# Attention, routing and two FFNs on one core: where spare weights are converted, when raw tiles are asked for, and how one-hot places are laid out

## Chip, cores and metric

One core of a Trainium2 chip. The metric is device time in microseconds of one execution; lower is better. The kernel before has a median of 944.61 us over three runs (944.56 to 945.29).

## The reference, cut to what matters

Three stages follow each other on 2304 tokens of 512 features.

```python
# 1. attention: 4 batches x 8 heads, 512 local and 32 global tokens, head size 64;
#    local queries see a window of +-32 keys and all global ones, global queries see everything
x = attention(q_l, k_l, v_l, q_g, k_g, v_g)          # -> [2304, 512]
# 2. mixture of 8 experts, 288 tokens each, greedy over all (token, expert) logits, largest first
logits = x @ w_gate
for idx in argsort(-logits.flatten()):
    tok, e = idx // 8, idx % 8
    if assigned[tok] < 0 and counts[e] < 288: assigned[tok] = e; counts[e] += 1
out[assigned == e] = relu(x[assigned == e] @ w1[e]) @ w2[e]      # w1: 512x1024, w2: 1024x512
# 3. gated FFN on every token, hidden size 1536
return (silu(x @ w_gate) * (x @ w_val)) @ w_out
```

All inputs and the output are fp32.

## The kernel before

**Matmuls.** In the FFN stages each fp32 product is made of three fp32r matmuls (`mm3`, L1000 to L1002): a weight tile is split into a high and a low part, and so is the activation; high x high, high x low and low x high are accumulated. The split of a weight tile of 128 x 1024 is done in `parts`: ScalarE copies the raw tile into the high half (L971) and VectorE subtracts it from the raw tile for the low half (L972). Tokens of an expert come as 272 + 16: 272 columns per matmul in the products (`TE`), the 16 left over of each expert are gathered in `rest`.

**Attention (`attention`).** 40 units (4 local blocks of 128 queries and one global unit for each half batch) run in a software pipeline: slot `n` issues the scores of unit `n`, the exponentials of `n-1`, the transposes of `n-2` and the product with V of `n-3`. Three more slots drain it. At the end of slots 3 and 6 to 42 the slot calls `cv.step()`, `int(CVA*(n+1)) - int(CVA*n)` times (`CV0`, `CV1`).

**Conversion (`Convert`).** The third stage's weights are 36 pieces of 128 x 1024 words. Each is read (`cv_raw`, 512 KB), packed by ScalarE (L116, `cv_a`) and three VectorE operations (L122 to L124, `cv_f`) and stored into a DRAM buffer `wd` (256 KB), from which the FFN reads it later. A generator walks through the pieces; a step is either the first VectorE operation of a piece (cost 0.6) or its other two (cost 1.2), with the loads, the ScalarE operation and the store of neighbouring pieces before or after them. In attention pieces 0 to `NC`-1 are converted, with three loads ahead (`LD`) and 5, 3 and 4 buffers. `second`, called between attention and the experts, runs whatever steps are left and then sets up pieces `NC` to 35 with one load ahead and two buffers of each kind (`rest_of`). In the FFN each `tick` adds `CV2` to a budget, once expert 1 has its tokens, and steps are taken while the budget is positive:

```python
s.cvw += n                                   # n = CV2, in convert()
while s.cvw > 0 and not s.cv.finished:
    s.cvw -= s.cv.step()
```

**Experts and FFN (`Ffn`).** `moe(k)` runs expert `k`: 8 blocks `h` of the first product and 6 of 8 blocks `y` of the second, each 12 matmuls and one tick, then 48 matmuls without a tick. `group(g)` runs the gated FFN for two experts at once: 12 blocks with four ticks of 12 matmuls each, then the output product with 512 columns per matmul (12 or 13 ticks). The order is expert 0, 1, group 0, expert 2, 3, group 1 and so on. A tick also takes the next steps of `bgen`, which interleaves the routing of the next experts (`Router.phase`), the gathers of their tokens (`fetch`) and the clean-up after each.

**Weight tiles.** All tiles stand in one list of 136 in order of use: 8 for each expert, 12 for `g` and `v`, 6 for `o`. `w` calls `pump(m)` when tile `m` is used: tiles up to `m` that are not yet split are split now; then at most one more is split ahead, up to `LOOK` = 4 past `m`, if it is `here`: asked at least `LAG` ticks ago, and for an expert's tile its routing finished. Then `load` asks for raw tiles: while fewer than `RAWS` past the next tile to be split are under way. There are `RAWS` = 4 raw buffers, and SyncE issues all these DMAs in program order, those of the conversion among them. Before the first expert three tiles are asked for (`LA0`).

```python
return m in s.raw and s.ticks - s.asked[m] >= LAG and (kind in "gvo" or s.done_phase >= k)
```

**Routing (`Router.phase`).** For each expert six rounds narrow down a threshold; a round is a comparison on VectorE (L677), 17 matmuls with one-hot weights `ohr` (L684) and some small VectorE operations. Then each chosen token gets a place. The place's low 7 bits become a one-hot row of 128 for each of 17 chunks: a comparison of an iota with the places on VectorE (L731), with the chunk innermost in memory (`ol` is [128, 128, 18]; `iota2` repeats the iota so that both operands are bf16), in two pieces of 8 and 10 chunks. 17 matmuls use `ol[:, :, c]`, a column step of 18 elements, as weights (L735) and give the token numbers, by which GpSimd gathers the rows (L872).

Of the kernel before, what the change touches and what calls it, by code (L numbers as in the profile page):

```python
# [9 lines left out]
F32 = mybir.dt.float32  # L10
F32R = mybir.dt.float32r
BF16 = mybir.dt.bfloat16
I32 = mybir.dt.int32
AF = mybir.ActivationFunctionType
ALU = mybir.AluOpType
# [10 lines left out]
NCH = 17  # L26
# [33 lines left out]
class Ctx: pass  # L60


CVA = 1.45
VW = 3
CV0, CV1 = 3, 6
QB = 8
PL = 2
RAWB, CB, FB, LD = 5, 3, 4, 3
NC = 24
EN = 36  # L70
UO, LW = 0, 39
ORD, KQN = 'hc4vgq56w', 2
# [2 lines left out]
class Convert:  # L75

    def __init__(s, tc, t, wd, pool):
        s.nc, s.t, s.wd = tc.nc, t, wd
        s.use(pool, RAWB, CB, FB)
        s.jobs = []  # L80
        for j in range(6):
            for nm in ("moe2_w_gate", "moe2_w_val"):
                s.jobs += [(nm, j, h) for h in range(2)]
        for j in range(6):
            s.jobs += [("moe2_w_out", j, h) for h in range(2)]
        s.raw, s.a, s.f = {}, {}, {}
        s.stored, s.finished = -1, False
        s.g = s.gen(0, NC, LD, False)

# [3 lines left out]
    def rest_of(s, pool):  # L93
# [3 lines left out]
        s.finished = False  # L97
        s.g = s.gen(NC, 36, 1, True)

    def load(s, n):  # L100
        nm, j, h = s.jobs[n]
        w = s.t[nm].bitcast(I32)
        raw = s.pool.tile([128, 512, 2], I32, name="cv_raw", bufs=s.rawb)
        if nm == "moe2_w_out":
            src = w[256 * j + 128 * h:256 * j + 128 * h + 128, :]
            dst = raw.rearrange("p n u -> p (n u)")
        else:
            src = w[256 * h:256 * h + 256, 512 * j:512 * j + 512].rearrange("(c p) f -> p c f", p=128)
            dst = raw.rearrange("p (c n) u -> p c (n u)", c=2)
        s.nc.sync.dma_start(dst, src)  # L110
        s.raw[n] = raw
# [52 lines left out]
def attention(tc, ctx, t, cv=None, consts=None, early=None):  # L164
    nc = tc.nc
    K = ctx
    with tc.tile_pool(name="a_c", bufs=1) as cp_, tc.tile_pool(name="a_w", bufs=3) as wp_, \
# [298 lines left out]
        for n in range(N + 3):  # L466
# [54 lines left out]
            if cv and n >= CV1:  # L521
                for _ in range(int(CVA * (n + 1)) - int(CVA * n)):
                    cv.step()
# [18 lines left out]
class Router:  # L542

    def __init__(s, tc, K, pool, bank=None):
        s.tc, s.nc, s.K, s.bank = tc, tc.nc, K, bank
        s.known = -1
        t = lambda shape, dt, name: pool.tile(shape, dt, name="r_" + name)
        s.pen = t([128, E], F32, "pen"); s.need = t([128, E], F32, "need"); s.nd = t([128, 1], F32, "nd"); s.sel8 = t([128, E], F32, "sel8")
        s.cap = t([128, E], F32, "cap"); s.w8 = t([128, E], F32, "w8"); s.w8p = t([128, 1], F32, "w8p")
        s.tk = t([128, NCH], F32, "tk"); s.ac = t([128, NCH], F32, "ac")  # L550
        s.Lm = t([128, NCH, E], F32, "Lm"); s.v = t([128, NCH], F32, "v"); s.v0 = t([128, NCH], F32, "v0")
        s.eq = t([128, NCH, E], F32, "eq")

        s.ohr = t([128, NCH, 4, 32], BF16, "ohr"); s.oh = s.ohr[:, :, 0, 0:E]
        s.T = t([128, KM], F32, "T"); s.io = [t([128, r, k], BF16, f"io{i}") for i, (k, r) in enumerate(KN)]; s.Td = t([128, max(k * r for k, r in KN)], F32, "Td"); s.cmp = t([128, NCH, KM], BF16, "cmp")
        s.ge = t([128, KM], BF16, "ge"); s.ke = t([128, 1], F32, "ke"); s.k1 = [t([128, 1], F32, f"k1{i}") for i in range(2)]
        s.onesb = t([128, 128], BF16, "onesb"); s.tri = t([128, 128], BF16, "tri"); s.iota = t([128, 128], F32, "iota")
        s.lo2 = [t([128, 1], F32, f"lo{i}") for i in range(2)]; s.k2 = t([128, 1], F32, "k2"); s.cd = t([128, 1], F32, "cd"); s.hi = t([128, 1], F32, "hi"); s.gmin = t([128, 1], F32, "gmin")
        s.mm = t([128, 2], F32, "mm"); s.mt = t([128, 2], F32, "mt")
        s.m1 = t([128, 1], F32, "m1"); s.d = t([128, 1], F32, "d"); s.ew = t([128, 1], F32, "ew"); s.em = t([128, 1], F32, "em")  # L560
        s.c8 = t([128, E], BF16, "c8"); s.e8 = t([128, E], F32, "e8"); s.ohe = t([128, E], F32, "ohe")
        s.eis = [t([128, 1], I32, f"ei{e}") for e in range(E)]; s.M = t([128, 2, NCH], F32, "M"); s.Mb = t([128, 2 * NCH], BF16, "Mb")
        s.ones = t([128, 2 * NCH], F32, "ones"); s.Pc = t([128, 2 * NCH + 2], BF16, "Pc")
        s.lo = t([128, NCH], I32, "lo"); s.thr = t([128, 4], F32, "thr")
        s.acc = t([128, NCH], F32, "acc"); s.pp = t([128, NCH], I32, "pp")
        s.hb = t([128, 4, NCH], F32, "hb"); s.h3 = t([128, 3, NCH], F32, "h3"); s.ol = t([128, 128, NCH + 1], BF16, "ol"); s.iota2 = t([128, 128, NCH + 1], BF16, "iota2"); s.lob = t([128, NCH + 1], BF16, "lob"); s.rid = t([128, NCH, 2], BF16, "rid")
        s.rh = t([128, NCH, 3, 2], BF16, "rh"); s.A = t([128, NCH], F32, "A"); s.G = t([128, NCH], F32, "G")
        s.idxf = [t([128, 3], F32, f"idxf{e}") for e in range(E)]
        s.idx = [t([128, 3], I32, f"idx{e}") for e in range(E)]
# [82 lines left out]
    def phase(s, n):  # L652
        nc, V, K, b = s.nc, s.nc.vector, s.K, s.bank
# [61 lines left out]
        p = b[:, 320:354]  # L715
# [4 lines left out]
        V.scalar_tensor_tensor(s.pp, s.M[:, 0], -1.0, s.M[:, 1], op0=ALU.add, op1=ALU.add)  # L720
        W = nc.gpsimd if n == 0 else V
        V.tensor_scalar(s.lo, s.pp, 127, None, op0=ALU.bitwise_and)
        V.tensor_copy(s.lob[:, 0:NCH], s.lo)
        V.tensor_tensor(s.hb, s.pp[:, None, :].to_broadcast([128, 4, NCH]), s.thr[:, :, None].to_broadcast([128, 4, NCH]), op=ALU.is_ge)
        yield 1, 0.0
        W.tensor_tensor(s.h3, s.hb[:, 0:3], s.hb[:, 1:4], op=ALU.subtract)
# [1 line left out]
                        s.rid[:, :, None, :].to_broadcast([128, NCH, 3, 2]), op=ALU.mult)  # L728
        for c0, c1 in ((0, 8), (8, NCH + 1)):
            yield 1, 0.0  # L730
            V.tensor_tensor(s.ol[:, :, c0:c1], s.iota2[:, :, c0:c1], s.lob[:, None, c0:c1].to_broadcast([128, 128, c1 - c0]), op=ALU.is_equal)  # L731
        yield TQ, 0.0
        q = b[:, 384:390]
        for c in range(NCH):
            nc.tensor.matmul(q, s.ol[:, :, c], s.rh[:, c].rearrange("p k u -> p (k u)"), start=c == 0, stop=c == NCH - 1)  # L735
        q3 = q.rearrange("p (k u) -> p k u", u=2)
        V.tensor_copy(s.idxf[n], q3[:, :, 1])
        V.scalar_tensor_tensor(s.idx[n], q3[:, :, 0], 16.0, s.idxf[n], op0=ALU.mult, op1=ALU.add)
# [25 lines left out]
TE = CAP  # L764
OT = 4
GW, GL = 6, 12
CV2 = 0.75
LA0 = 3
MO = 1
YT = 0  # L770
GROUPS = [[0, 1], [2, 3], [4, 5], [6, 7]]
WB, LOOK, RAWS, LAG = 6, 4, 4, 2
class Ffn:
    def __init__(s, tc, K, R, pool, banks, t):
        s.tc, s.nc, s.K, s.R, s.t, s.pool = tc, tc.nc, K, R, t, pool
# [138 lines left out]
    def tick(s):  # L914
        s.ticks += 1
        if 1 in s.ready:
            s.convert(CV2)
        if s.wait > 0:
# [72 lines left out]

    def load(s):
        s.nd = max(s.nd, s.np)
        while s.nd < min(s.np + RAWS, len(s.tiles)) and s.known(s.nd):
            s.dma(s.nd)
            s.nd += 1

# [212 lines left out]
```

## Time and profile before

| | us |
|---|---|
| median of three runs | 944.61 |
| the profiled execution | 943.54 |
| its span | 941.7 |
| attention ends, last copy of the logits (L527) | 172.7 |
| first matmul of expert 0 | 205.5 |
| expert 1's first product with a split tile, on the chain of waits | 251.7 |
| expert 1's last eviction (L1050) ends | 292.7 |
| the last conversion operation on VectorE ends | 343.2 |

| engine | busy us | share of the span |
|---|---|---|
| TensorE, matmuls | 858.6 | 91% |
| VectorE | 590.9 | 63% |
| ScalarE | 394.0 | 42% |
| GpSimd | 107.2 | 11% |

Times in the trace are counted from the start of the span. Rows by stretch give the busy times in the order TensorE matmuls, TensorE weight loads, VectorE, ScalarE, GpSimd. In the trace's names PE is TensorE, PEld its weight loads, DVE is VectorE, ACT ScalarE, POOL GpSimd and SP SyncE; b are the PSUM banks, rbank the router's. The shares are means over stages with different limits, so the profile is read by stretch: how much of a stretch TensorE was busy, what the other engines did in it, and which waits ended last. A TensorE clock of 1.00 is 2.4 GHz; the lower of the two levels, 1.2 GHz, shows as 0.50, and a mean over a stretch that has both lies between.

### The profile page before, as it was taken

What the parts mean: (1) busy time and instruction counts of PE and PEld (TensorE: products, weight loads), DVE (VectorE), ACT (ScalarE), POOL (GpSimd) and SP (SyncE); (2) the same over time, 40 slices, a digit from 0 to 9 for tenths busy, and PEclk for the clock granted to TensorE, in tenths of its full rate; (3) what the DMA queues carried; (4) which work ended last, traced back from release to release, by engine and by line L of the source; (5) the groups of instructions that cost most, each with busy time, mean ns of one, the idle gap of its engine ahead of it and who ended that gap; (6) DMA issues with size and microseconds to landing.
All of it is one profiled execution on the core that took longest, in us unless ns stands there. A gap on an engine that the chain in (4) does not pass through costs nothing.

```text
span 941.7 us, 19213 instructions
## 1 busy us (share of the span) xinstructions
PE 858.6 (91%) x7567; PEld 794.8 (84%) x7567; DVE 590.9 (63%) x1489; ACT 394.0 (42%) x823; POOL 107.2 (11%) x189
## 2 busy tenths in 40 slices
PE   6999999448688678999999999999999999999997
PEld 5888887348588678978999889899999889999985
DVE  3678777678787687756896877355554336644410
ACT  4888887122343332323443233244443234533300
POOL 5444230010100100102100000110100020000002
PEclk9999999759699789999999999999999999999999
DMA  7988994041576532233651312365412435522101
GB/s 172 242 243 247 265 286 130 33 159 59 167 236 224 180 124 87 73 114 132 183 175 53 110 46 85 127 194 174 140 56 84 131 114 179 157 90 90 46 1 56
DMA packets 109386, 128.62 MB, mean 137 GB/s; under 512 B 57392, under 2 KB 75056, under 8 KB 109296
## 3 DMA queue, kind: packets, MB, share of 16 engines
q1 hardware_dynamic: 105856, 118.35, 41.2%
q0 software_dynamic: 2896, 8.92, 2.7%
q8 instruction: 59, 0.97, 0.4%
q14 instruction: 31, 0.25, 0.1%
q10 hardware_dynamic: 544, 0.13, 0.1%
HBM read 109.02 MB, written 18.35 MB: 135 GB/s over the span
## 4 chain that ended last, share of the span: by engine, by line
PE 53%; issue 20%; DVE 15%; DMA 4%; ACT 4%; POOL 1%; SPq 1%; POOLq 0%; DVEq 0%; ACTq 0%
PE b L1000 9%; PE b L1002 8%; PE b L1001 8%; PE b L1105 4%; PE b L1106 4%; PE b L1107 4%; DVE wHL L972 3%; PE s L303 3%; DMA wd<-cv_f 3%; DVE r_cmp L677 2%; PE tr L323 2%; PE o L334 2%; PE o L339 1%; PE tr L269 1%; PE tr L358 1%
## 5 line engine op out<-in xcount | busy, mean ns | idle before, releaser
L1000 PE MATMUL b<-yH,wHL 128*128 128x272 f32 x768 | 229.1, 298 | 0.4 <-DVE yL L1050 0.4
L1002 PE MATMUL b<-yH,wHL 128*128 128x272 f32 x768 | 225.2, 293 | 0.0
L1001 PE MATMUL b<-yL,wHL 128*128 128x272 f32 x768 | 224.7, 293 | 0.0
L972 DVE TENSOR_TENSOR wHL<-raw,wHL 128x1024 fp32r<-128x1024 f32 x136 | 163.8, 1222 | 45.0 <-ACT wHL L971 44.9
L971 ACT CAST wHL<-raw 128x1024 fp32r<-128x1024 f32 x136 | 139.2, 1047 | 79.3 <-PE b L1107 52.2
L1000 PEld LDWEIGHTS b<-yH,wHL 128*128 128x128 f32 x768 | 148.7, 194 | 8.5 <-issue 7.7
L1001 PEld LDWEIGHTS b<-yL,wHL 128*128 128x128 f32 x768 | 149.1, 194 | 0.0
L1002 PEld LDWEIGHTS b<-yH,wHL 128*128 128x128 f32 x768 | 148.6, 193 | 0.0
L1083 ACT CAST dH<-b 128x272 fp32r<-128x272 f32 x96 | 37.1, 386 | 187.5 <-DVE b L1082 187.5
L1082 DVE TENSOR_TENSOR b<-b,si 128x272 f32<-128x272 f32 x96 | 42.8, 446 | 55.8 <-PE b L1002 55.7
L1000 PE MATMUL b<-dH,wHL 128*128 128x272 f32 x256 | 76.1, 297 | 1.7 <-ACT dH L1027 1.7
L1000 PE MATMUL b<-xH,wHL 128*128 128x272 f32 x252 | 75.2, 298 | 1.6 <-DVE dL L1028 0.8
L1105 PE MATMUL b<-wHL,dH 128*128 128x512 f32 x192 | 76.4, 398 | 0.0
L1001 PE MATMUL b<-dL,wHL 128*128 128x272 f32 x256 | 74.7, 292 | 1.7 <-DVE dL L1028 1.7
L1002 PE MATMUL b<-xH,wHL 128*128 128x272 f32 x252 | 74.0, 294 | 2.2 <-DVE wHL L972 2.2
L1107 PE MATMUL b<-wHL,dH 128*128 128x512 f32 x192 | 75.9, 395 | 0.0
L1106 PE MATMUL b<-wHL,dL 128*128 128x512 f32 x192 | 75.9, 395 | 0.0
L1002 PE MATMUL b<-dH,wHL 128*128 128x272 f32 x256 | 74.5, 291 | 0.0
L1001 PE MATMUL b<-xL,wHL 128*128 128x272 f32 x252 | 73.4, 291 | 0.0
L1084 DVE TENSOR_TENSOR dL<-b,dH 128x272 fp32r<-128x272 f32 x96 | 42.4, 442 | 43.5 <-ACT dH L1083 43.5
L1027 ACT ACTIVATE dH<-b 128x272 fp32r<-128x272 f32 x64 | 25.4, 397 | 95.5 <-PE b L1002 89.4
L872 POOL DMA_INDIRECT xg<-xd,r_idx x24 | 22.8, 949 | 309.5 <-DVE r_idxf L739 123.1
(236 smaller groups left out, 1610.8 us busy)
## 6 DMA issues: line engine op xcount, KB each, us to landing
raw<-wd SPq DMA_DIRECT2D x72, 512.0 KB, 3.6
raw<-moe_w SPq DMA_DIRECT2D x64, 512.0 KB, 4.0
wd<-cv_f SPq DMA_DIRECT2D x36, 256.0 KB, 5.4
cv_raw<-moe_w_gate SPq DMA_DIRECT2D x12, 512.0 KB, 4.7
cv_raw<-moe_w_val SPq DMA_DIRECT2D x12, 512.0 KB, 5.8
cv_raw<-moe_w_out SPq DMA_DIRECT2D x12, 512.0 KB, 6.6
xd<-xt SPq DMA_DIRECT2D x16, 256.0 KB, 4.6
st<-k_l SPq DMA_DIRECT2D x28, 128.0 KB, 4.8
```

The lines of the kernel that those rows point to most:

```text
L303: nc.tensor.matmul(s[:, u, 160 * a:160 * a + 160], qT[n % 2][:, a, 2 * g + u].rearrange("d h q -> d (h q)"), kT[n % 2][:, a, o:o + 160], s ...
L971: nc.scalar.copy(w[:, 0], raw)
L972: nc.vector.tensor_tensor(w[:, 1], raw, w[:, 0].bitcast(F32), op=ALU.subtract)
L1000: nc.tensor.matmul(out, wH, xH, start=start, stop=False)
L1001: nc.tensor.matmul(out, wH, xL, start=False, stop=False)
L1002: nc.tensor.matmul(out, wL, xH, start=False, stop=stop)
L1082: nc.vector.tensor_tensor(b, b, si, op=ALU.mult)
L1083: nc.scalar.copy(dH[:, f, :], b)
L1084: nc.vector.tensor_tensor(dL[:, f, :], b, dH[:, f, :].bitcast(F32), op=ALU.subtract)
L1105: nc.tensor.matmul(ob[i], dh, H[:, f % 2, :], start=f == 0, stop=False)
L1106: nc.tensor.matmul(ob[i], dl, H[:, f % 2, :], start=False, stop=False)
L1107: nc.tensor.matmul(ob[i], dh, L[:, f % 2, :], start=False, stop=f == 11)
```

## The change

Seven constants and conditions and the layout of one tile are changed. Attention takes 1.65 conversion steps per slot and converts 30 of the 36 pieces; the FFN takes 0.4 budget units per tick. A raw tile must have been asked for four ticks ago to be split ahead, and `load` asks up to two tiles past the next one to be split and not three; the number of raw buffers stays. For experts 1 to 7 the one-hot places are written with the place innermost (`olc`, a view of the same memory), from the fp32 iota and the int32 places, in pieces of 8 and 9 chunks, and the matmuls read contiguous weights; the bf16 copy of the places (`lob`) is made for expert 0 only.

```diff
-CVA = 1.45
+CVA = 1.65
-NC = 24
+NC = 30
...
+        s.olc = s.ol.rearrange("p w c -> p (w c)")[:, 0:NCH * 128].rearrange("p (c w) -> p c w", w=128)
...
-        V.tensor_copy(s.lob[:, 0:NCH], s.lo)
+        if n == 0:
+            V.tensor_copy(s.lob[:, 0:NCH], s.lo)
...
-            V.tensor_tensor(s.ol[:, :, c0:c1], s.iota2[:, :, c0:c1], s.lob[:, None, c0:c1].to_broadcast([128, 128, c1 - c0]), op=ALU.is_equal)
+            if n == 0:
+                V.tensor_tensor(s.ol[:, :, c0:c1], s.iota2[:, :, c0:c1], s.lob[:, None, c0:c1].to_broadcast([128, 128, c1 - c0]), op=ALU.is_equal)
+            else:
+                x = slice(c0, min(c1, NCH))
+                N = x.stop - c0
+                V.tensor_tensor(s.olc[:, x], s.iota[:, None, :].to_broadcast([128, N, 128]), s.lo[:, x, None].to_broadcast([128, N, 128]), op=ALU.is_equal)
...
-            nc.tensor.matmul(q, s.ol[:, :, c], s.rh[:, c].rearrange("p k u -> p (k u)"), start=c == 0, stop=c == NCH - 1)
+            nc.tensor.matmul(q, s.olc[:, c] if n else s.ol[:, :, c], s.rh[:, c].rearrange("p k u -> p (k u)"), start=c == 0, stop=c == NCH - 1)
...
-CV2 = 0.75
+CV2 = 0.4
-WB, LOOK, RAWS, LAG = 6, 4, 4, 2
+WB, LOOK, RAWS, LAG = 6, 4, 4, 4
...
-        while s.nd < min(s.np + RAWS, len(s.tiles)) and s.known(s.nd):
+        while s.nd < min(s.np + RAWS - 1, len(s.tiles)) and s.known(s.nd):
```

## Rows read from the trace of the kernel before

**Rows 1.** stretches: length, busy us of each engine, granted clock, DMA share, GB/s

```profile
20.00:146.70 126.70, 125.90 (x1699) 108.60 (x1700) 93.44 (x213) 108.91 (x295) 45.86 (x89) 1.00 0.88 251
...
205.50:251.70 46.20, 35.38 (x346) 33.06 (x346) 39.09 (x135) 13.81 (x23) 2.77 (x3) 0.83 0.26 82
...
251.70:292.70 41.00, 35.67 (x307) 34.28 (x308) 34.24 (x90) 20.27 (x31) 0.00 (x0) 0.89 0.72 227
...
292.70:345.50 52.80, 36.70 (x274) 36.11 (x273) 37.72 (x90) 14.92 (x32) 2.76 (x3) 0.81 0.59 194
...
345.50:620.00 274.50, 265.06 (x2155) 246.77 (x2155) 194.72 (x574) 91.81 (x167) 23.48 (x32) 0.98 0.34 106
...
620.00:941.70 321.70, 315.14 (x2230) 298.86 (x2228) 141.84 (x217) 118.01 (x216) 14.57 (x23) 1.00 0.34 107
```

**Rows 2.** waits, 251.7 to 345.5 us: total us, times, longest us

```profile
ACT cv_a L116 <- DMA cv_raw<-moe_w_out: 21.6, 5, 5.9
...
DVE cv_f L122 <- DMA wd<-cv_f: 10.6, 4, 4.9
```

**Rows 3.** chain of waits, second expert: start us, us, what

```profile
295.82 7.23 DMA wd<-cv_f
```

**Rows 4.** chain of waits, first expert, first and last of 23 matmuls

```profile
226.40 0.12 PE b L1001
...
229.17 0.14 PE b L1002
```

**Rows 5.** DMA issues: count, KB each, median us from issue to landing

```profile
raw<-moe_w SPq DMA_DIRECT2D x64, 512.0 KB, 4.0
...
wd<-cv_f SPq DMA_DIRECT2D x36, 256.0 KB, 5.4
...
cv_raw<-moe_w_out SPq DMA_DIRECT2D x12, 512.0 KB, 6.6
```

**Rows 6.** groups by line, VectorE, 292 to 345 us: busy us, mean ns

```profile
L972 DVE TENSOR_TENSOR wHL<-raw,wHL 128x1024 fp32r<-128x1024 f32 x6 | 7.1, 1220 | 1.3 <-ACT wHL L971 1.3
...
L124 DVE SCALAR_TENSOR_TENSOR cv_f<-cv_raw,cv_f 128x512 int32<-128x512 int32 x8 | 5.5, 692 | 0.3
...
L123 DVE SCALAR_TENSOR_TENSOR cv_f<-cv_a,cv_f 128x512 int32<-128x512 int32 x8 | 5.5, 684 | 0.1
...
L122 DVE TENSOR_SCALAR cv_f<-cv_raw 128x512 int32<-128x512 int32 x8 | 3.4, 421 | 8.1 <-DMA wd<-cv_f 8.1
...
L724 DVE TENSOR_TENSOR r_hb<-r_pp,r_thr 128x68 f32<-128x68 int32 x1 | 0.2, 222 | 0.0
```

**Rows 7.** chain of waits, groups 0 and 1: one-hot and router matmuls

```profile
386.78 1.06 PE rbank L735 x17
...
432.14 0.45 PE rbank L684 x17
```

**Rows 8.** stretches, whole core, 4 and 20 us with a full VectorE

```profile
220.00:224.00 4.00, 3.14 (x38) 3.14 (x38) 3.91 (x9) 0.24 (x1) 0.00 (x0) 1.00 0.00 0
...
460.00:480.00 20.00, 19.74 (x195) 19.36 (x194) 18.06 (x47) 9.70 (x16) 0.27 (x1) 1.00 0.57 172
```

**Rows 9.** timeline, VectorE, end of attention: start, us, operation [idle before]

```profile
163.00 0.17 DVE L344 TENSOR_SCALAR rd<-o 128x4 f32<-128x4 f32 x1 [1.24 <-PE o L339]
...
165.31 0.16 DVE L344 TENSOR_SCALAR rd<-o 128x4 f32<-128x4 f32 x1 [1.47 <-PE o L339]
...
167.87 0.17 DVE L344 TENSOR_SCALAR rd<-o 128x4 f32<-128x4 f32 x1 [1.73 <-PE o L339]
```

**Rows 10.** groups by line, TensorE weight loads, whole run

```profile
L684 PEld LDWEIGHTS <-r_ohr 128*128 128x128 bf16 x714 | 22.4, 98 | 27.1 <-issue 24.7
...
L735 PEld LDWEIGHTS <-r_ol 128*128 128x128 bf16 x136 | 9.2, 162 | 7.3 <-DVE r_ol L731 5.8 <-issue 1.2
```

**Rows 11.** timeline, VectorE, the one-hot comparison of expert 2

```profile
305.23 0.69 DVE L731 TENSOR_TENSOR r_ol<-r_iota,r_lob 128x1024 bf16<-128x1024 bf16 x1
...
307.42 0.82 DVE L731 TENSOR_TENSOR r_ol<-r_iota,r_lob 128x1280 bf16<-128x1280 bf16 x1
```

More of the change, by code (lines that the diff above doesn't have):

```diff
@@ L565, in __init__ @@
         s.acc = t([128, NCH], F32, "acc"); s.pp = t([128, NCH], I32, "pp")
-        s.hb = t([128, 4, NCH], F32, "hb"); s.h3 = t([128, 3, NCH], F32, "h3"); s.ol = t([128, 128, NCH + 1], BF16, "ol"); s.iota2 = t([128, 128, NCH + 1], BF16, "iota2"); s.lob = t([128, NCH + 1], BF16, "lob"); s.rid = t([128, NCH, 2], BF16, "rid")
+        s.hb = t([128, 4, NCH], F32, "hb"); s.h3 = t([128, 3, NCH], F32, "h3"); s.ol = t([128, 128, NCH + 1], BF16, "ol"); s.iota2 = t([128, 128, NCH + 1], BF16, "iota2"); s.lob = t([128, NCH + 1], BF16, "lob")
+        s.olc = s.ol.rearrange("p w c -> p (w c)")[:, 0:NCH * 128].rearrange("p (c w) -> p c w", w=128); s.rid = t([128, NCH, 2], BF16, "rid")
         s.rh = t([128, NCH, 3, 2], BF16, "rh"); s.A = t([128, NCH], F32, "A"); s.G = t([128, NCH], F32, "G")
```

## The prediction

> **What bounds the kernel now.** The stretches come first [rows 1]. From 620 us on TensorE is busy 315.1 of 321.7 us; in attention (20 to 146.7 us) it is busy 125.9 of 126.7 us. What is lost lies between: 46.2 us for the first expert and the hand-over to the second with TensorE busy 35.4 us, and then two stretches of 41.0 and 52.8 us with 35.7 and 36.7 us of it, at mean granted clocks of 0.89 and 0.81. In these last two (251.7 to 345.5 us, 93.8 us: the second expert and the first 22 ticks of group 0) the kernel converts its last twelve weights. The waits there [rows 2] have two entries that belong to nothing but this conversion: ScalarE stands 21.6 us in five waits for `cv_raw` loads, VectorE 10.6 us in four waits for `cv_f` stores. Both engines work in order, so the evictions and splits that TensorE waits for stand behind. The chain of waits shows it: single `wd<-cv_f` stores on it, 7.23 us in the one shown [rows 3].
>
> The cause is in the numbers of the planner. A weight costs 0.6 + 1.2 = 1.8 units, a tick pays 0.75: a weight every 2.4 ticks. A tick is 12 matmuls; their pitch is 0.126 us (of 23 in a row on the chain the first and last start at 226.40 and 229.17 us [rows 4]: 2.77/22), so 1.51 us, and 2.4 ticks are 3.6 us. The loads take 6.6 us and the stores 5.4 us to land [rows 5]. With one load ahead and two buffers that can't fit.
>
> **Six weights out of the FFN, at a slower pace.** At 0.4 a tick a weight comes every 4.5 ticks, 6.8 us: longer than both landings. Counting the generator through: first load at tick 15, words at ticks 25 to 48, finished at tick 51 (before: words at 20 to 47, finished at 49). Six words in place of twelve take 6 x (0.421 + 0.684 + 0.692) = 10.8 us from VectorE [rows 6].
> The TensorE work of the stretch: the 3-matmul products in it are 456 (22 ticks and the 192 of the expert), 57.5 us; the router's matmuls about 5 us (seven rounds of 17 at 0.45 us [rows 7] and some small ones); 3 us I allow for the lower clock at its start. That is 65.5, the floor. VectorE was busy 34.2 + 37.7 = 71.9 us [rows 1]; less 10.8, plus 0.9 for the one-hot of expert 2 (below), it is 62.0. What TensorE does beside so full a VectorE is seen at 460 to 480 us: VectorE 18.06 of 20, TensorE 19.74 [rows 8]. At that 0.90 the stretch needs 62.0/0.90 = 69 us; I add 3.5 us, because two loops (evictions, router rounds) share VectorE in order and loads of 6.6 us against 6.8 us leave short waits. So 72.3 in place of 93.8: **-21.5 us**. Bounds: -28.3 (the floor), and -10.8 if only VectorE's work goes and each stall comes back as another.
>
> **Six weights into attention.** The slots: int(1.45 x 43) - int(1.45 x 6) + 1 = 55 steps, of which 50 were used; with 1.65 there are 70 - 9 + 1 = 62, and 2 x 30 + 2 = 62 are needed. So the conversion just ends in attention's last slot, and nothing is left to be flushed ahead of the router. VectorE gets 10.8 us more, ScalarE six activations of 512 elements, the DMA 6 x 768 KB = 4.72 MB. The room between 20 and 146.7 us: VectorE 33 us, ScalarE 18 us, DMA 0.12 of 126.7 us = 15 us [rows 1]; at 251/0.88 = 285 GB/s the 4.72 MB need 16.5 us, some of it after 146.7. While TensorE has no gap this is hidden. It is not in the drain after the last unit, where VectorE is on the chain: up to the last `mx` one operation of 0.42 us comes on top (the old slots hold three words there, the new ones three and the first operation of a fourth); then 1.80 us of conversion fall into a VectorE gap of 1.24, 1.38 into 1.47, 1.80 into 1.73 [rows 9]. Sum 0.42 + 0.56 + 0 + 0.07 = 1.1; I take **+2.2**, as much again for units inside attention that VectorE makes late. Bounds: 0 (work is only added, so no gain) and 16.5 (the DMA full).
>
> **Plain order of one-hot places, experts 1 to 7.** TensorE: the weights of the 17 matmuls are now contiguous columns. Loading a strided one-hot takes 162 ns, the contiguous one-hot of the router's rounds 98 ns, both 128 columns of bf16 [rows 10]; on the chain 17 matmuls of the first kind take 1.06 us, of the second 0.45 us [rows 7]. So -0.61 each. By a rule of the Trainium skill (page "TensorE: Matmul & The Clock Gate", section "Weight-path perf modes — Fast Weight Load (FWL) and DoubleRow") non-fp32 weights of 128 columns load fast at any column step up to about a thousand elements. By that the step of 18 elements would cost nothing and the TensorE gain be 0; the trace's 162 against 98 ns speaks against it here, and the measurement decides.
> VectorE: the comparison reads fp32 and int32 where it read bf16. Before, 1024 and 1280 elements took 0.69 and 0.82 us [rows 11]; 1024 fp32 elements take 1.22 us [rows 6], so 1024 and 1152 take 1.22 + 1.37. An int32 operand alone costs nothing visible (L724, 68 elements in 222 ns [rows 6]). Less a small copy (about 0.18, like L724): +0.9 us each. Expert 1: TensorE's queue of matmuls runs through it, so -0.6 on the path from routing to gather. Expert 2 is in the stretch above. Experts 3 to 7: five times -0.61 where TensorE has no gap, less about 1 us where VectorE holds it up (345.5 to 620 us has 9.4 us of idle TensorE [rows 1]). Sum **-2.7**; bounds -4.3 (7 x 0.61) and +6.3 (no TensorE gain, all of VectorE's).
>
> **Raw tiles later, and four ticks of age.** Counted through the pump's rule, tile by tile: with the old numbers only tiles 0, 1 and 8 are split at the moment of use; with the new ones tile 2 too (`w2` of expert 0 at tick 3: asked at -1, so not old enough at tick 2). Its ScalarE copy and VectorE subtraction (the latter 1.22 us [rows 6]) then stand between two products. VectorE is the bound there (3.91 of 4 us [rows 8]) and does the same splits in both orders, three ticks later; what it loses is its idle time in ticks 0 to 2 and during that copy: **+1.7**, bounds -1 (the router's rounds start sooner) and +2.5. For experts 2 to 7 the age of a raw tile at its split falls from 8.1 ticks on average (6 at least) to 6.1 (4 at least, 6.0 us), against 4.0 us of landing [rows 5]: hidden; the split still stands 6 ticks or more ahead of use. The load that is no longer asked for had to wait on SyncE for the splitting just issued, with conversion loads and stores behind it; that gain is in the -21.5.
>
> **Sum.** The profiled execution took 943.54 us (span 941.7): 943.54 - 21.5 + 2.2 - 2.7 + 1.7 = 923.2. The median of the runs shown is 1.07 us above that execution, so 924.3, rounded to 924.
>
> **Rivals.**
> *Attention pays for it.* For: ScalarE is busy 108.9 of 126.7 us, the DMA 0.88. Against: TensorE has no gap, and 33 us of VectorE are free. If all of the 10.8 us shows in place of 2.2: 933; with a full DMA 938.6.
> *The stalls change hands.* Evictions, router rounds and splits share VectorE in order, and only the removed work counts, -10.8: 935. For: after 345.5 us, without any conversion, TensorE still idles 9.4 us. Against: 32 us of waits carry the conversion's name.
> *The plain order saves TensorE nothing.* The step between columns is not what costs the 162 ns, 17 matmuls stay at 1.06 us and VectorE's 1 us is paid: -2.7 becomes +1, so 928. For: both loads are 128 columns of bf16. Against: the 98 ns [rows 10]. The rule of the Trainium skill named above is this rival.
> *Raw tiles come too late (slower).* ScalarE meets a raw tile that hasn't landed, and in order behind it stand the evictions. It decides from a landing over 6.0 us (the age of the youngest), where 18 of 48 expert tiles have an age of 5 ticks or less, and over 9.1 us for all. Then a wait of 0.5 us at each of 48 tiles is 24 us and the time 924.3 + 24 = 948. Against: 4.0 us is the median, and each tile is split 6 ticks before its use.
>
> **Chances.** Forecast 0.62 (915 to 931), attention 0.12, stalls 0.13, no TensorE gain 0.08, raw tiles 0.05. A change of 0.2% (1.9 us) is about what a measurement tells from none. Faster: the first four, less 0.04 of the two costlier ones that could eat everything together: 0.91; same 0.03; slower 0.06. The range takes in the forecast's own, the 928, the 933 and most of the 935: 913 to 936, leaving out the DMA-full end and the slower case.
>
> **What would show it.** Between the first product of expert 1 and the end of the conversion: some 72 us, with no waits of ScalarE for `cv_raw` and of VectorE for `wd` over 2 us in sum. The logits' last copy (172.7 us now) 1 to 3 us later. The 17 one-hot matmuls of experts 1 to 7 in 0.45 us. One split at use in expert 0. From 620 us of now on, the same lengths. It is wrong if attention grows by over 6 us, or if TensorE idles over 12 us in the stretch that now idles 21.4.

## The result and the profile after

The kernel after takes 931.66 us (median of four runs, 931.21 to 932.46), the kernel before 944.59 (four runs, 943.29 to 945.29): ratio 0.9863, 95% interval 0.9846 to 0.9881. The forecast was 924, its range 913 to 936. The time lies in the range, 7.7 us above the forecast. The step that carried the sum came out as predicted; two small ones were several times too small. Times of one profiled execution move from run to run, those of attention most (below).

The profiled execution took 931.21 us, span 929.4. Both traces are cut at the same events, so that the differences add up to that of the spans, 12.3 us:

| from, to | before | after | change | forecast |
|---|---|---|---|---|
| start, logits' last copy (end of attention) | 172.69 | 180.90 | +8.2 | +2.2 |
| to expert 0's first product (routing, gather) | 32.78 | 33.80 | +1.0 | 0 |
| to expert 1's first product from split tiles | 43.18 | 46.58 | +3.4 | +1.1 |
| to tick 22 of group 0 | 96.59 | 75.99 | -20.6 | -21.5 |
| to group 1's output product | 232.82 | 227.50 | -5.3 | -2.1 with the next row |
| to group 3 | 243.06 | 242.51 | -0.6 | |
| to the end | 120.61 | 122.13 | +1.5 | 0 |

The stretches of after; the columns are those of [rows 1], the ends are moved with the work:

```profile
20.00:146.70 126.70, 121.42 (x1606) 104.45 (x1605) 94.10 (x212) 103.40 (x278) 45.31 (x89) 0.98 0.88 256
214.70:261.30 46.60, 36.04 (x344) 34.14 (x344) 37.08 (x126) 12.64 (x22) 2.77 (x3) 0.83 0.28 92
261.30:295.40 34.10, 30.05 (x278) 28.71 (x278) 28.12 (x79) 15.44 (x23) 0.00 (x0) 0.89 0.53 167
295.40:337.30 41.90, 37.55 (x304) 36.88 (x303) 35.72 (x84) 17.40 (x34) 3.10 (x3) 0.92 0.58 186
```

In attention TensorE now has 5.3 us of gaps where before it had 0.8, and ScalarE did less in the same 126.7 us (103.4 for 108.9), not more: something was late. The stretches of expert 1 and group 0 before, from the same matmuls on as the last two rows above; [rows 1] cut them 3 to 5 us later:

```profile
248.66:288.12 39.46, 32.35 (x278) 30.85 (x278) 32.63 (x87) 16.80 (x26) 0.00 (x0) 0.85 0.71 225
288.12:345.25 57.13, 40.62 (x304) 39.82 (x303) 41.98 (x102) 19.27 (x37) 2.76 (x3) 0.83 0.57 187
```

In these two stretches VectorE is busy 63.8 us where it was busy 74.6, and TensorE idles 8.4 us of 76.0 where it idled 23.6 of 96.6. All waits there that a transfer ends, in the trace of after, 261.3 to 337.3 us (total us, times, longest us):

```profile
ACT wHL L979 <- DMA raw<-wd: 1.3, 2, 0.7
```

The 21.6 us on `cv_raw` and the 10.6 us on `wd` of [rows 2] are gone. But in attention, where such waits summed to 0.2 us before, ScalarE now stands for `cv_raw`. Waits of after, 20 to 172 us:

```profile
ACT cv_a L116 <- DMA cv_raw<-moe_w_val: 9.2, 5, 4.2
ACT xT L360 <- PE tr L358: 4.9, 12, 0.8
...
ACT cv_a L116 <- DMA cv_raw<-moe_w_gate: 1.3, 2, 1.1
```

The chain of waits of after shows what they delay (start us, us, what): TensorE's products, then a load, then the exponentials (`p`) that stood behind it on ScalarE.

```profile
71.25 1.09 PE s L303 x8
73.49 0.69 ACT ptb L324 x2
74.17 4.21 DMA cv_raw<-moe_w_val
79.03 1.25 ACT p L314 x4
...
136.24 6.75 DMA cv_raw<-moe_w_val
143.59 1.23 ACT p L314 x4
```

Why was that load late? SyncE's own rows of after (start, duration, line, transfer, count): from 126 to 137 us the queue is held throughout, the eight transfers of one half batch's values hold it 5.83 us, and the load at 136.24 comes 10 us after the one before it.

```profile
126.00 0.55 SPq L110 DMA_DIRECT2D cv_raw<-moe_w_val  x1
126.59 0.47 SPq L128 DMA_DIRECT2D wd<-cv_f  x1
127.17 5.83 SPq L210 DMA_DIRECT2D TA<-v_l  x8
133.23 0.31 SPq L212 DMA_DIRECT2D TA<-v_g  x1
133.63 0.58 SPq L419 DMA_DIRECT2D xd<-gx  x1
134.25 1.23 SPq L201 DMA_DIRECT2D st<-q_l  x2
135.58 0.56 SPq L350 DMA_DIRECT2D xd<-xt  x1
136.24 0.40 SPq L110 DMA_DIRECT2D cv_raw<-moe_w_val  x1
```

The row of eight is not issuing alone. In this program SyncE's transfers use eight semaphores in turn, and in attention each one stands until the transfer eight places before it has landed. The seventh value transfer here stands 1.7 us (up to 132.12) for the load that was issued at 126.00. SyncE's waits for landings at the value transfers of after, 20 to 172 us, sum to some 10 us (before: some 7):

```profile
SPq L210 <- DMA cv_raw<-moe_w_gate: 3.3, 4, 1.8
SPq L210 <- DMA cv_raw<-moe_w_out: 3.2, 3, 1.7
SPq L210 <- DMA wd<-cv_f: 2.1, 4, 1.2
SPq L210 <- DMA cv_raw<-moe_w_val: 1.7, 1, 1.7
```

In expert 0 one split now stands at its use. TensorE, after (bracket: idle before, and what ended it): the second operand of a product waits for VectorE's subtraction, and then matmuls start 0.23 us apart instead of 0.126 [rows 4]: the granted clock is 0.50.

```profile
222.71 0.39 PE L1009 MATMUL b<-dH,wHL 128*128 128x272 f32 x1 [0.99 <-ACT wHL L979]
222.94 0.29 PE L1010 MATMUL b<-dL,wHL 128*128 128x272 f32 x1
225.51 0.59 PE L1011 MATMUL b<-dH,wHL 128*128 128x272 f32 x1 [2.29 <-DVE wHL L980]
225.90 0.43 PE L1009 MATMUL b<-dH,wHL 128*128 128x272 f32 x1
226.13 0.43 PE L1010 MATMUL b<-dL,wHL 128*128 128x272 f32 x1
```

VectorE, the engine that bounds this part, runs dry behind it:

```profile
224.24 2.35 DVE L980 TENSOR_TENSOR wHL<-raw,wHL 128x1024 fp32r<-128x1024 f32 x2
231.33 0.44 DVE L1037 SCALAR_TENSOR_TENSOR dL<-b,dH 128x272 fp32r<-128x272 f32 x1 [4.74 <-ACT dH L1036]
```

The one-hot places, after: weight loads of the 17 matmuls (min/median/max ns; 17 of the 136 are expert 0's, still strided), the comparison that writes them, and one place on the chain. They answer [rows 7, 10, 11].

```profile
L743 PEld LDWEIGHTS <-r_ol x136: 95/96/164, 201.6 to 598.9; 128*128 128x128 bf16 x136
...
L739 DVE TENSOR_TENSOR r_ol<-r_iota,r_lo x14: 1215/1282/1352, 248.2 to 589.8; 128x1024 bf16<-128x1024 f32 x7, 128x1152 bf16<-128x1152 f32 x7
```

```profile
446.65 0.44 PE rbank L743 x17
```

### The profile page after: what moved, and what is told of

Its sections match the earlier page's. It is cut to its first block, busy times and chain, and to the rows that moved or that the text cites. A ratio compares the mean times of both kernels' runs of the same rounds, so it can differ in the third digit from the quotient of the medians.

```text
span 929.4 us, 19215 instructions
## 1 busy us (share of the span) xinstructions
PE 852.3 (92%) x7567; PEld 787.9 (85%) x7567; DVE 595.3 (64%) x1482; ACT 393.8 (42%) x823; POOL 110.5 (12%) x189
## 4 chain that ended last, share of the span: by engine, by line
PE 52%; issue 21%; DVE 17%; ACT 4%; DMA 3%; SPq 1%; POOL 1%; POOLq 0%; DVEq 0%; ACTq 0%
PE b L1009 9%; PE b L1011 9%; PE b L1010 8%; PE b L1114 4%; PE b L1115 4%; PE b L1116 4%; DVE wHL L980 3%; PE s L303 2%; DVE r_cmp L678 2%; PE tr L323 2%; DMA cv_raw<-moe_w_val 2%; PE o L334 2%; DVE b L1091 1%; ACT dH L1092 1%; PE o L339 1%
## 5 line engine op out<-in xcount | busy, mean ns | idle before, releaser
L1009 PE MATMUL b<-yH,wHL 128*128 128x272 f32 x768 | 226.5, 295 | 0.1
L1011 PE MATMUL b<-yH,wHL 128*128 128x272 f32 x768 | 222.9, 290 | 0.0
L1010 PE MATMUL b<-yL,wHL 128*128 128x272 f32 x768 | 222.3, 290 | 0.0
L980 DVE TENSOR_TENSOR wHL<-raw,wHL 128x1024 fp32r<-128x1024 f32 x136 | 163.7, 1222 | 41.0 <-ACT wHL L979 40.2
L1009 PEld LDWEIGHTS b<-yH,wHL 128*128 128x128 f32 x768 | 146.2, 190 | 5.4 <-issue 5.0
L1010 PEld LDWEIGHTS b<-yL,wHL 128*128 128x128 f32 x768 | 146.6, 191 | 0.0
L1011 PEld LDWEIGHTS b<-yH,wHL 128*128 128x128 f32 x768 | 146.2, 190 | 0.0
L1011 PE MATMUL b<-xH,wHL 128*128 128x272 f32 x252 | 74.6, 296 | 3.5 <-DVE wHL L980 3.4
L880 POOL DMA_INDIRECT xg<-xd,r_idx x24 | 25.7, 1072 | 296.7 <-DVE r_ac L754 104.6
```

Source lines behind the costliest of these rows:

```text
L880: nc.gpsimd.indirect_dma_start(out=xg[0:n, blk, :], out_offset=None, in_=s.K.xd[:, :], in_offset=bass.IndirectOffsetOnAxis(ap=s.R.idx[k][0 ...
L980: nc.vector.tensor_tensor(w[:, 1], raw, w[:, 0].bitcast(F32), op=ALU.subtract)
L1009: nc.tensor.matmul(out, wH, xH, start=start, stop=False)
L1010: nc.tensor.matmul(out, wH, xL, start=False, stop=False)
L1011: nc.tensor.matmul(out, wL, xH, start=False, stop=stop)
```

## Experiments

Two questions came from the trace. For attention, theory A: SyncE, which issues in order, gets to the loads of pieces too late (in e1 and e2 because of the added transfers, from e5 on because pieces are asked for faster); B: the added bytes fill the DMA engines; C: the added operations of VectorE and ScalarE hold up the units. For expert 0, whether the age of 4 costs what that one split costs. Ratios are to runs of the kernel before on the same chip (944.16, 944.18 and 944.62 us), with 95% intervals; they are not the quotients of the medians (in e5 1.0032 against 1.0056). Differences in us are of medians; by the ratios e3's gain over after is 7.5 us, e4's 10.0 and e9's 4.6. Stage lengths are of one profiled execution each. Attention with the code of after ended at 178.0 to 186.1 us in five of them, with the code of before at 172.7 and 172.9 in two, so its growth of 8.2 us is one value of a band.

**The added transfers (e1, e2).** In the kernel after, pieces 24 to 29 take the words of piece 23 and are neither loaded nor stored, and three output tiles read other stored pieces. In e2 twelve tiny transfers stand in their places.

```diff
+        if 24 <= n < NC:
+            s.extra_load(n)
+            return
...
+    def extra_load(s, n):
+        s.raw[n] = s.raw[23]
```

> The changed kernel without the twelve transfers that the six added pieces bring into attention: pieces 24 to 29 are made from the words of piece 23, neither loaded nor stored, and three output tiles read other stored pieces (so the output is not the reference's). ScalarE's and VectorE's work stays. The logits' last copy is at 180.9 us in the changed kernel and 172.7 us before. Theory A (SyncE's queue is full, the twelve issues delay the loads behind them): 174 to 176 us, and the time falls by 5 to 7 us to 925 to 927. Rival B (the DMA engines are full): the same here. Rival C (VectorE's and ScalarE's added 10.8 and 4 us, in order, hold up the units): still 180 to 181 us and 931 to 932.

> As the kernel without transfers, but with twelve transfers at the same places of SyncE's queue that move 8 bytes per partition each and not 4096 or 2048: the issues are back, the 4.7 MB are not. Theory A (issues): the logits' last copy at 179 to 181 us, as in the changed kernel. Rival B (bytes): 174 to 176 us. Rival C: 180 to 181 us, as without transfers.

e1: 932.18 us (0.9863, 0.9822 to 0.9904), logits at 180.6. e2: 930.55 (0.9846, 0.9808 to 0.9885), 179.4. Without the six pieces' transfers nothing changes: e1 came out as expected under C, and A's twelve transfers and B fall. e2 does not part A from C, given the band. But C alone does not explain the waits, which are still there (7.6 us in 4, 6.6 in 5), at pieces below 24. The pace reaches all pieces, so the next runs looked at the queue as a whole.

**Values of a half batch by five transfers (e3).** The kernel after; same bytes, and nothing changed on ScalarE and VectorE.

```diff
-            for h in range(4):
-                for p0, p1, c, x in ((32, 128, 0, 0), (0, 32, 1, 96 * D)):
-                    nc.sync.dma_start(v[p0:p1, c:c + 4, h, 0:64], bass.AP(tensor=vl.tensor, offset=o + h * SL * D + x, ap=[[D, p1 - p0], [128 * D, 4], [1, D]]))
+            for c in range(5):
+                p0, p1 = (32 if c == 0 else 0), (32 if c == 4 else 128)
+                nc.sync.dma_start(v[p0:p1, c, :, 0:64], bass.AP(tensor=vl.tensor, offset=o + (128 * c + p0 - 32) * D, ap=[[D, p1 - p0], [SL * D, 4], [1, D]]))
```

> The changed kernel with the V rows of a half batch loaded by 5 transfers (one per block of 128 keys) and not 8 (two per head): the same bytes in the same 256-byte rows, 24 issues fewer on SyncE over attention, some 14 us of its queue at about 0.6 us each. Theory A: the waits of ScalarE for cv_raw go, the logits' last copy at 173.5 to 176 us, the time 924 to 927 us. Rivals B and C: 180 to 181 us and 931 to 932.

925.97 us (0.9784, 0.9744 to 0.9825), logits at 175.9. This is what A expected and C did not. The block of value transfers holds SyncE 4.5 us in the mean of seven half batches instead of 5.7, and the waits of ScalarE on `cv_raw`, 20 to 172 us, are

```profile
ACT cv_a L116 <- DMA cv_raw<-moe_w_val: 0.4, 1, 0.4
```

The DMA share is not lower than in after (0.93, 0.96, 0.93 in the 40 us stretches from 20 us on, against 0.80, 0.90, 0.92): the transfers had room, the queue that issues them had none. What the five transfers save on it is mainly standing for landings, 2.4 us where after had 10.3:

```profile
SPq L210 <- DMA cv_raw<-moe_w_out: 1.9, 2, 1.3
SPq L210 <- DMA wd<-cv_f: 0.5, 2, 0.3
```

Over before 3.2 us are left, but that sets five transfers against eight; like with like (e10 below, 171.1) it is 4.8. On the chain of waits from 20 to 170 us, conversion operations of VectorE (`cv_f`) take 9.0 us in e3 and 4.0 in e10. So a part of C stands beside A; no run takes VectorE's added work away.

**Pace alone (e5).** The kernel before with `CVA` 1.65 and nothing else.

> The kernel before with one constant changed, the pace of weight pieces per tick of attention (CVA 1.45 to 1.65); still 24 pieces, and nothing else of the change. In the kernel after, the logits' last copy came at 180.9 us instead of 172.7. Theory A (pace): the same pieces asked for sooner in attention stand behind a SyncE queue that is already issuing back to back, ScalarE waits for cv_raw, and the logits' last copy comes at 177 to 181 us, with 5 to 19 us of ScalarE waits on cv_raw before 170 us. Rival B (number): it is the six further pieces that lengthen attention, so with 24 the copy stays at 172 to 174 us and no such wait appears. In either case the total is not below that of the kernel before by more than 2 us, since the stretch behind attention still has its 12 later pieces.

949.43 us (1.0032, 1.0008 to 1.0056), logits at 177.8. The waits on `cv_raw`, 20 to 172 us:

```profile
ACT cv_a L116 <- DMA cv_raw<-moe_w_val: 8.2, 5, 2.7
```

So the waits and 5.1 us come with the pace alone, at the same 24 pieces: the rival (only the number of pieces counts) falls. How much the number adds is not resolved within the band.

**Five transfers without the pace (e10).** The kernel before with the edit of e3.

> The kernel before with the values of a half batch loaded by five transfers instead of eight, and nothing of the change. Theory A (the queue's issue time matters only because the pieces are asked for faster): ScalarE had 0.2 us of waits on cv_raw in attention before, so there is nothing to win: logits' last copy at 171.5 to 173.5 us and the time within 2 us of before. Rival: fewer, larger transfers shorten attention whatever the pace; then the copy comes at 170 us or sooner and the time falls by 3 to 6 us, and what the same edit gave in the kernel after (6 us) was no loss of the change.

943.04 us (0.9979, 0.9965 to 0.9993), logits at 171.1. A gain of 1.6 us where after gained 5.7: by the medians most of what e3 won back was lost by the change, a smaller part is to be had at any pace.

**Age 2 for all tiles (e4), and for tile 2 alone (e9).**

```diff
-WB, LOOK, RAWS, LAG = 6, 4, 4, 4
+WB, LOOK, RAWS, LAG = 6, 4, 4, 2
```

```diff
-        return m in s.raw and s.ticks - s.asked[m] >= LAG and (kind in "gvo" or s.done_phase >= k)
+        return m in s.raw and s.ticks - s.asked[m] >= (2 if m == 2 else LAG) and (kind in "gvo" or s.done_phase >= k)
```

> The changed kernel with the age for splitting ahead back at two ticks. Theory D (the third tile of expert 0, split at the moment of use, stops TensorE for 2.3 us and brings the lower clock after it): from the first product of expert 0 to that of expert 1 43 to 44 us (46.6 in the changed kernel, 43.2 before), the time 928 to 930 us. Rival E (the later ask for raw tiles is what costs there): 46 to 47 us, 931 to 932.

> The kernel after with the age back to 2 for one tile alone, tile 2 of expert 0 (its first w2 tile); every other tile keeps age 4. With age 2 for all tiles the time was 921.34 us, and expert 0's stage 42.1 us instead of 46.6. Theory: the whole of it is that one split, which age 4 forces at its use, in the middle of expert 0's first products, where TensorE stands for it and the granted clock falls; so here expert 0's stage is 42 to 43.5 us and the time 921 to 925 us. Rival: every split of the stretch that comes two ticks later costs a little; then expert 0's stage is 44 to 46 us, the next two stages stay at 34 and 42 us, and the time is 927 us or more.

e4: 921.34 us (0.9757, 0.9723 to 0.9791), less than D expected. e9: 926.89 (0.9814, 0.9790 to 0.9839), with expert 0's stage at 41.3 us instead of 46.6 and the next two unchanged at 34.1 and 41.8. In e9 TensorE does not stand, and its clock stays; 4 us stretches of after, where the split stood and the clock fell, and of e9:

```profile
222.00:226.00 4.00, 1.01 (x4) 0.79 (x5) 3.82 (x12) 1.60 (x2) 0.00 (x0) 0.80 0.00 0
226.00:230.00 4.00, 4.00 (x20) 4.00 (x20) 0.59 (x1) 0.00 (x0) 0.00 (x0) 0.50 0.74 243
```

```profile
223.00:227.00 4.00, 4.00 (x47) 3.94 (x47) 3.78 (x12) 1.78 (x4) 0.00 (x0) 1.00 0.48 135
227.00:231.00 4.00, 4.00 (x45) 3.76 (x44) 3.82 (x12) 2.74 (x4) 0.00 (x0) 1.00 0.38 131
```

Both theories of e9 hold in part. Tile 2 is worth 4.8 us, all of expert 0's loss and more. Of the other 5.5 us of e4, 3.3 stand in the profiles at the later splits of expert 1 and group 0: those stages take 32.5 and 40.2 us in e4. The remainder is within the intervals.

**Raw tiles asked for as early as before (e8).** e4 with the third part of the change wholly undone.

```diff
-        while s.nd < min(s.np + RAWS - 1, len(s.tiles)) and s.known(s.nd):
+        while s.nd < min(s.np + RAWS, len(s.tiles)) and s.known(s.nd):
```

> The kernel after with the raw tiles asked for as early as before (RAWS, not RAWS - 1) and the age back to 2: the third part of the change undone, the other two kept. With the age alone undone it was 921.34 us. Theory: asking one tile later matters only by when SyncE's queue holds its transfers and is worth 1 us or less, so 920 to 923 us here. Rival: the later ask is what frees the stretch behind attention of waits on raw tiles; then 924 us or more, with the loss between expert 1 and the middle of group 0.

922.80 us (0.9782, 0.9730 to 0.9834): 1.5 us over e4, less than the intervals, and the stretch from expert 1 to tick 22 is 73.1 us against 72.7. The later ask is worth little or nothing; the rival falls.

**Old order of one-hot places (e7).** The kernel after with `ol[:, :, c]` and the bf16 comparison for all experts.

> The kernel after with the one-hot places of all experts in the old order (bf16, strided weight loads); the pieces, the age and the raw ask stay changed. Theory: the plain order takes some 0.6 us from TensorE in each of the 17 places of the later experts (1.06 to 0.45 us) and costs VectorE about 1 us per expert that lies beside other work, so without it the time is 2 to 5 us longer, 933.5 to 936.5 us, and it is lost behind expert 0, not in attention. Rival: the dearer comparison on VectorE takes back what TensorE saves, or the one-hot products lie beside waits anyway; then the time is that of the kernel after, within 1 us (930.5 to 932.5).

933.40 us (0.9869, 0.9822 to 0.9915), 1.7 us over after: between theory and rival by the median, and the interval (some 4 us to either side) can't tell them. The trace is clearer. The same 136 matmuls, strided, in e7:

```profile
L742 PEld LDWEIGHTS <-r_ol x136: 139/163/165, 207.3 to 607.4; 128*128 128x128 bf16 x136
```

```profile
453.51 1.07 PE rbank L742 x17
```

Where TensorE has no gap the stages show it whole: expert 2 takes 27.14 us in e7 and 26.50 in after, group 1's output product to expert 4 takes 34.86 and 34.22. That is 0.64 us for one place, against 0.61 predicted.

**Five transfers and age 2 together (e6), and all 36 pieces in attention on top (e11).**

```diff
-CVA = 1.65
+CVA = 1.95
-NC = 30
+NC = 36
```

> The kernel after with two edits, each of which was run by itself before: the values of a half batch loaded by five transfers instead of eight (925.97 us by itself), and the age from which an unused split is forced back to 2 (921.34 us by itself). If the two act in different stretches (attention; expert 0 to the middle of group 0) their gains add: logits' last copy at 175 to 176 us, expert 0's stage at 42 us, 914 to 919 us in all. If the second gain came from the same waits as the first (the attention of that run was 2.9 us shorter too, without an edit there), the sum stays at 919 to 922 us.

> The kernel after with values loaded by five transfers and the age back to 2 (both together 921.42 us), and all 36 pieces instead of 30 in attention, at a pace of 1.95 instead of 1.65. If a further piece in attention costs 0.4 us (2.7 us for the six) and saves what it cost in the stretch from expert 1 to the middle of group 0 (72.4 us there now), the time is 915 to 920 us. Rival: attention has no room left at this pace, ScalarE and VectorE delay TensorE's products: logits' last copy at 182 us or later, and 922 us or more.

e6: 921.42 us (0.9759, 0.9720 to 0.9797); e11: 921.47 (0.9757, 0.9733 to 0.9782). Neither beats e4, and both missed what was expected. In the profiles of e6 and e4 attention is 2.7 us shorter in e6, routing and gather 1.5 us longer, and the rest 0.9 us shorter; why the 5.7 us of e3 do not come again is open. In e11 the waits are back, the logits come at 180.9, and what the later stages win (70.3 for 72.4 us up to tick 22, and less behind it) is spent:

```profile
ACT cv_a L116 <- DMA cv_raw<-moe_w_gate: 7.2, 5, 2.9
```

**The pieces undone (e12).** The kernel after with `CVA` 1.45, `NC` 24, `CV2` 0.75.

> The kernel after with the first part undone: 24 pieces at a pace of 1.45 in attention, CV2 0.75; the plain one-hot order, the age of 4 and the later ask stay. If the terms are those that the stages have shown (the age costs 4 to 8 us, the plain order gives back 2 to 3), the time is 946 to 950 us, and the six pieces are then worth 14 to 18 us. By the terms of the prediction (the age and the ask +1.7, the plain order -2.7) it is 942 to 944 us, and the pieces are worth 11 to 12 us.

942.54 us (0.9980, 0.9961 to 0.9998). The pieces are worth 10.9 us. That is the smaller of the two sums, so the stage terms do not simply add. The profiled execution (946.29 us, above its median) shows expert 0's stage at 47.5 us, as dear as in after, but the stretch up to tick 22 at 93.2 us, 3.4 shorter than before. An age that costs 10 us with 30 pieces costs little with 24, as far as these runs tell; that a stretch which waits for transfers anyway takes later splits for nothing is a reading of mine, and no run isolates it.

## Why the prediction held, and where it failed

**Six weights out of the FFN: right, in size and in reason.** -20.6 us for -21.5; waits for `cv_raw` and `wd` gone, 8.4 us of idle TensorE where 12 was the bound of failure. The forecast's stretch starts at the third matmul of expert 1 (251.66 us before, 264.29 after); from there it is 73.0 us for a forecast of 72.3. (The description says 48 matmuls behind an expert's last tick; by the code they are 24, as the forecast's 192 counts them.) VectorE is busy 0.84 of the stretch; that it sets the floor is read from this share, no run tests it. Nor does a run part the smaller number of weights from the slower pace there. The rival that stalls change hands falls.

**Six weights into attention: the step that failed, +8.2 for +2.2.** By the prediction's own test (over 6 us) it was wrong. It weighed the load on VectorE, ScalarE and the DMA and found room in each. For the DMA that was right: in e1 the bytes cost nothing. It did not look at the queue that issues the transfers, though every load of the conversion goes through it; before the change, rows of issuing already covered 106 of SyncE's 126.7 us (20 to 146.7). The six pieces were priced as work added, while the edit also brings all other pieces forward: 1.65 steps where there were 1.45. Behind 4.1 to 6.7 us of value transfers a load then comes too late, and ScalarE, in order, holds the exponentials for which TensorE waits. The 1.1 us of the drain did not show: from the last score matmul to the logits' last copy it is 14.6 us before and 13.9 after. "As much again for units inside attention" was too small: with five transfers in both kernels, where ScalarE hardly waits for `cv_raw`, the change still costs 4.8 us. So in these single profiles the queue accounts for some 3 to 5 of the 8.2 us; the rest fits VectorE's added work but is not shown to be it. Of the rivals, attention's was the nearest in place and size (933 against 931.66), and perhaps partly in its reason.

**Age and ask: the second, +1.7 predicted; undoing the age is worth 10.3.** The one split at use was named, at the right tile and tick. What it costs was mis-sized: only VectorE's idle time was counted, not that TensorE stands 3 us and is then granted half its clock for some 5 us. At a pitch of 0.23 instead of 0.126 us the 21 matmuls up to 230.67 us cost 2 us more by themselves. And the splits of expert 1 and group 0, for which it had no price, cost 3.3 us more in the profiles. The profile of e4 also shows a shorter attention by 2.9 us, which its code does not explain, so the size of the whole is softer than that of tile 2.

**Plain order: right in each place.** 0.61 us a place forecast, 0.64 seen; the whole (-2.7) is not resolved, e7 gives 1.7 by the median; VectorE's comparisons 1.22 and 1.35 us for 1.22 and 1.37. The rival falls: with a step of 18 elements a weight load takes 163 ns, contiguous 96, in otherwise equal matmuls (e7 and after). The Trainium skill ("TensorE: Matmul & The Clock Gate", "Weight-path perf modes — Fast Weight Load (FWL) and DoubleRow") allows its fast weight load a column step of up to 1,024 elements, so that by it both would load alike; here the measurement decides.

**Not forecast: -3.8 us in group 1.** Its first products take 90.9 us before and 87.2 after. The kernels with 24 pieces have 89.5 to 92.3 us there, those with 30 or 36 have 86.8 to 87.5, with either order of places and either age: it comes with the first part of the change (the number of pieces, with the pace in the FFN). Before, two parts of it ran below full clock (0.94 and 0.96); after, all at 1.00. Trace of before, then of after:

```profile
510.00:540.00 30.00, 27.96 (x257) 27.55 (x256) 23.31 (x72) 9.28 (x20) 2.76 (x3) 0.94 0.32 106
540.00:578.10 38.10, 36.14 (x324) 35.34 (x323) 28.19 (x93) 12.12 (x27) 0.60 (x1) 0.96 0.17 56
```

```profile
500.50:530.50 30.00, 26.97 (x265) 26.49 (x264) 24.88 (x73) 9.66 (x21) 3.38 (x3) 1.00 0.30 107
530.50:564.80 34.30, 32.94 (x314) 31.98 (x312) 26.99 (x85) 11.66 (x26) 0.60 (x1) 1.00 0.20 62
```

How a conversion that ends in group 0 reaches group 1 was not tried and stays open. It covered over 3 us of what the other steps missed.

## What to carry to other kernels

When work is moved into a stage that looks to have room, ask of each queue, and not only of each engine, whether it has a gap and how many transfers it may have under way, and price a faster pace for all of the work that it brings forward. A forced step in the middle of a run of matmuls costs the stall, the lower clock behind it, and what starves downstream: count all three. And when a forecast comes out near, compare it stage by stage: here misses of 6.0, 2.3, 1.5 and 1.0 us were partly covered by a gain of over 3 us that nobody had forecast.

## What the runs showed of the hardware

The granted clock fell once with no gap on TensorE in the trace. In after, at the start of group 3, TensorE is busy throughout and is granted 0.72 and then 0.50 for some 3.4 us; the stage is 1.5 us longer than before. It took 73.8 us in nine of the fourteen profiled executions and 72.3 in five; e4 and e8, whose code for group 3 is the same but for the ask, are on either side.

```profile
805.00:807.30 2.30, 2.30 (x21) 2.14 (x20) 0.88 (x2) 1.94 (x4) 0.00 (x0) 1.00 0.51 207
807.30:809.00 1.70, 1.70 (x11) 1.70 (x11) 1.62 (x3) 0.60 (x1) 0.00 (x0) 0.72 0.00 0
809.00:811.00 2.00, 2.00 (x11) 2.00 (x10) 0.94 (x1) 0.40 (x1) 0.00 (x0) 0.50 0.07 23
```

A queue with room for eight transfers under way pays for many small ones. The same bytes of values hold SyncE for 4.1 to 6.7 us as eight transfers (after) and for 2.8 to 5.7 us as five (e3). The low ends are one half batch without waits, 4.12 and 2.79 us, so issuing itself is a part; in most of the others eight stand longer for earlier landings.
